# A weight-streaming recurrence on one core: a deeper ring, a different choice of resident chunks, an early preload, and four small moves

## The chip, the cores and the metric

One core of one Trainium2 chip. The metric is the device time of one execution in microseconds. Every run quoted here is in the fast state, so all of them may be compared; the sessions used different chips, so between sessions I compare the ratios to the kernel before, which ran in the same rounds. The kernel before takes 2934.2 us (median of 15 runs, 2922.1 to 2950.2).

## The reference, cut to what matters

Two independent computations on sequences of 2048 x 1024, in bf16. Part A is a gated long convolution through FFTs. Part B is a recurrent transformer: 64 segments of 32 tokens, each with 8 memory tokens in front that are the previous segment's output, so no segment can begin its projections of the memory rows before the last one is finished.

```python
for s in range(n_seg):                       # 64 segments
    h = concatenate([mem, x[s*32:(s+1)*32]])  # 8 + 32 tokens
    q = h @ Wq; k = h @ Wk; v = h @ Wv        # 32 heads of 128, each weight 8 MB
    p = softmax(mask(q @ k.T * scale))
    o = (p @ v) @ Wo                          # 8 MB
    mem = o[:8]; outs.append(o[8:])
```

The four weights are 32 MB together. The kernel keeps a part of them in on-chip memory and reads the rest again in each segment.

## The kernel before: the parts concerned

Part A has three stages: A1 (shifted product, first half of the FFT), A2 (34 units of complex product and second transform), A3 (last transform, gate, output). Part B cuts the weights into 64 chunks of 512 KB, 16 per matrix. 38 of them are resident; the other 26 are loaded anew in every segment, in order of use, by the SP queue into a ring of tiles. A load can only be issued when TensorE has finished with the tile that the ring gives it.

```python
NRES = 38; RING = 6
nres = [NRES // 4 + (1 if m < NRES % 4 else 0) for m in range(4)]   # Wq,Wk,Wv,Wo = 10,10,9,9
# ... the n resident chunks of a matrix are spread evenly over its 16 places ...
for m in range(4):                       # all residents first, ahead of the first segment
    for i in range(NCH):
        if i in res_slot[m]:
            nc.sync.dma_start(dst_view(res_tiles[m][:, res_slot[m][i], :], m), dram_chunk(m, i))

def wchunk(m, i):
    if i in res_slot[m]:
        return res_tiles[m][:, res_slot[m][i], :]
    t = ring.tile([128, CW], BF, tag="wring", name="wchunk")
    nc.sync.dma_start(dst_view(t[:], m), dram_chunk(m, i))
    return t[:]
# ... one segment: Q pass, K pass, V pass (beside it the scores and softmax), OTp, Wo pass ...
```

In the names of the profile, `acc` are the sums of the Q, K and V passes, `yacc` that of the Wo pass, `OTp` is attention times V, `PTs` the transposed softmax. In every fourth segment a pass works on two batches of rows (the "double" segments below).

In A2 each unit has four products on VectorE, then

```python
nc.gpsimd.tensor_tensor(out=Yre[P_], in0=pa[P_], in1=pb[P_], op=ALU.subtract)
nc.vector.tensor_tensor(out=Yim[P_], in0=pc[P_], in1=pd[P_], op=ALU.add)
```

## Time and profile before

| | before |
|---|---|
| median | 2934.2 us |
| profiled span, mean TensorE clock | 2931.5 us, 0.830 |
| first matmul of part B | at 282.8 us |
| end of the first segment (copy of its Y) | at 370.7 us |
| each of the other 63 segments | 40.35 us |
| from the last copy of Y to the end | 18.5 us |

The last three rows come from the starts of ScalarE's copies `Y_sb<-yacc` in the trace: 370.68 us for the first, 2912.96 us for the last, and their difference over 63. A segment is then cut by ScalarE's other events in it: end of the last copy of QA, of KA, starts of the two exponentials, first copy of OT, last copy of OT, end of the copy of Y. Means over the 63 segments, with TensorE's busy time, clock and DMA rate of the same stretches:

| stretch, before | us | PE busy us | clock | GB/s |
|---|---|---|---|---|
| Q: Y to end of QA | 10.98 | 6.85 | 0.883 | 369 |
| K: to end of KA | 8.43 | 6.76 | 0.854 | 359 |
| to first exponential | 4.62 | 4.14 | 0.963 | 381 |
| softmax, rest of V, to first OT | 7.21 | 3.58 | 0.873 | 377 |
| OTp | 2.81 | 2.78 | 0.521 | 283 |
| Wo: to Y | 6.30 | 5.82 | 0.746 | 234 |

The profile's own lines of before are shown in the prediction.

### The profile page before, as it was taken

Reading aid. Unit: us, or ns where it says so; the run is one execution under the profiler, and the core shown is the slowest. Engines: PE = TensorE matmul, PEld = TensorE weight load, DVE = VectorE, ACT = ScalarE, POOL = GpSimd, SP = SyncE. Lnnn points to the kernel's source line nnn. Section 1 sums busy time; section 2 is a strip of 40 time slices with the busy share of each in tenths; the row PEclk is TensorE's granted clock in tenths of the full one; section 3 lists DMA queues with packets and bytes.
Section 4 is the critical chain, followed back from the end, with each engine's and each line's share of the span. In section 5 each row is a group of like instructions: output and inputs, shape, how many; then the busy total and the mean of one; then the engine's idle time right before and its main releaser. Section 6 shows DMA issues by size and latency. Waiting matters only on the chain.

```text
span 2931.5 us, 80956 instructions
## 1 busy us (share of the span) xinstructions
PE 2079.3 (71%) x36052; PEld 1131.4 (39%) x36052; DVE 924.4 (32%) x1936; ACT 631.8 (22%) x1191; POOL 378.8 (13%) x714
## 2 busy tenths in 40 slices
PE   3665467686777778776867777777767786777775
PEld 1221234343444434343434444343434343443433
DVE  6895122232222322222322222222223222222222
ACT  6771111111111111111211111121112111111111
POOL 4141001001010101010010101010100101010101
PEclk9796689888887879788888888897979888897977
DMA  7886999989999999999999999999999999999996
GB/s 243 305 303 237 366 343 330 341 322 359 352 328 346 334 348 341 360 330 346 342 358 357 336 349 335 350 342 334 331 350 334 358 355 331 353 337 343 344 349 236
DMA packets 356981, 979.09 MB, mean 334 GB/s; under 512 B 42556, under 2 KB 47708, under 8 KB 356631
## 3 DMA queue, kind: packets, MB, share of 16 engines
q1 hardware_dynamic: 329896, 942.33, 88.5%
q0 software_dynamic: 21504, 21.04, 2.2%
q10 hardware_dynamic: 5232, 10.55, 1.2%
q8 instruction: 282, 4.62, 0.6%
q14 instruction: 67, 0.55, 0.1%
HBM read 940.19 MB, written 33.55 MB: 332 GB/s over the span
## 4 chain that ended last, share of the span: by engine, by line
PE 41%; DMA 32%; DVE 14%; ACT 4%; issue 2%; POOL 1%; SPq 0%; ACTq 0%; DVEq 0%; POOLq 0%
DMA wchunk<-in_B_Wq_dram 19%; PE acc L536 18%; PE yacc L561 11%; DMA wchunk<-in_B_Wk_dram 8%; PE OTp L698 4%; PE OTp L701 3%; PE qk_tp L548 3%; DMA wchunk<-in_B_Wv_dram 3%; DVE Ppads L592 2%; DVE ssum L590 2%; ACT KA_sb L541 2%; DVE mx L586 2%; ACT QA_sb L541 1%; DVE SA L582 1%; DVE SA L587 1%
## 5 line engine op out<-in xcount | busy, mean ns | idle before, releaser
L536 PE MATMUL acc<-wchunk,hT 128*32 128x512 bf16 x4864 | 583.7, 426 | 404.1 <-DMA wchunk<-in_B_Wq_dram 188.8
L536 PE MATMUL acc<-Wres,hT 128*32 128x512 bf16 x7424 | 771.8, 426 | 5.1 <-DMA Wres<-in_B_Wq_dram 5.1
L536 PEld LDWEIGHTS <-hT 128*32 128x32 bf16 x12288 | 393.6, 102 | 871.6 <-issue 646.1
L549 DVE COPY QT_sb<-qk_tp 128x1024 bf16<-128x1024 bf16 x80 | 55.3, 692 | 779.2 <-PE qk_tp L548 779.2
L698 PE MATMUL OTp<-PTs,VA_sb 32*128 32x64 bf16 x2048 | 202.1, 229 | 134.2 <-DVE PTs L687 132.6
L561 PEld LDWEIGHTS <-OT_sb 128*32 128x32 bf16 x8192 | 259.8, 121 | 80.9 <-issue 8.2
L561 PE MATMUL yacc<-Wres,OT_sb 128*32 128x256 bf16 x4608 | 289.1, 338 | 0.1
L561 PE MATMUL yacc<-wchunk,OT_sb 128*32 128x256 bf16 x3584 | 261.5, 352 | 6.7 <-DMA wchunk<-in_B_Wo_dram 3.9
L698 PEld LDWEIGHTS <-VA_sb 32*128 32x128 bf16 x2048 | 177.8, 118 | 184.9 <-issue 155.2
L536 PE MATMUL acc<-Wres,hTB 128*32 128x512 bf16 x1856 | 239.9, 386 | 0.0
L721 POOL DMA_DIRECT2D out_dram<-Y_sb x256 | 128.2, 508 | 841.1 <-ACT Y_sb L565 555.0
L541 ACT CAST QA_sb<-acc 128x512 bf16<-128x512 f32 x128 | 73.8, 588 | 673.5 <-PE acc L536 673.5
L605 POOL COPY hT<-XT_sb 128x192 bf16<-128x192 bf16 x64 | 22.2, 347 | 1437.0 <-issue 1053.1
L549 DVE COPY KT_sb<-qk_tp 128x1024 bf16<-128x1024 bf16 x80 | 55.2, 689 | 464.3 <-PE qk_tp L548 464.3
L701 PE MATMUL OTp<-PTs,VB_sb 32*128 32x64 bf16 x2048 | 193.5, 230 | 0.7
L541 ACT CAST KA_sb<-acc 128x512 bf16<-128x512 f32 x128 | 75.2, 588 | 489.4 <-PE acc L536 489.4
L701 PEld LDWEIGHTS <-VB_sb 32*128 32x128 bf16 x2048 | 179.5, 120 | 0.0
L536 PE MATMUL acc<-wchunk,hTB 128*32 128x512 bf16 x1216 | 168.8, 387 | 1.1 <-issue 1.1
L536 PEld LDWEIGHTS <-hTB 128*32 128x32 bf16 x3072 | 130.6, 98 | 70.8 <-issue 6.9
L704 ACT CAST OT_sb<-OTp 128x256 bf16<-128x256 f32 x256 | 94.3, 372 | 268.3 <-PE OTp L701 268.2
L612 DVE COPY hT<-mt_tp 128x64 bf16<-128x64 bf16 x64 | 12.3, 191 | 402.3 <-PE mt_tp L611 402.3
L726 POOL DMA_DIRECT2D out_dram<-YB_sb x256 | 126.6, 501 | 68.5 <-DMA out_dram<-Y_sb 30.6
(206 smaller groups left out, 2239.2 us busy)
## 6 DMA issues: line engine op xcount, KB each, us to landing
wchunk<-in_B_Wv_dram SPq DMA_DIRECT2D x448, 512.0 KB, 6.9
wchunk<-in_B_Wo_dram SPq DMA_DIRECT2D x448, 512.0 KB, 7.4
wchunk<-in_B_Wq_dram SPq DMA_DIRECT2D x384, 512.0 KB, 7.1
wchunk<-in_B_Wk_dram SPq DMA_DIRECT2D x384, 512.0 KB, 8.2
SK<-s_sb SPq DMA_DIRECT2D x16, 512.0 KB, 4.7
SU<-s_sb SPq DMA_DIRECT2D x16, 512.0 KB, 3.6
Kg<-SK ACTq DMA_DIRECT2D x32, 256.0 KB, 4.5
Ug<-SU SPq DMA_DIRECT2D x32, 256.0 KB, 5.0
```

The lines of the kernel that those rows point to most:

```text
L536: nc.tensor.matmul(accs[pi][g][32 * c:32 * c + 32, :], lhsT=hT_ap[:, kc, :], rhs=w[:, jl * 512:(jl + 1) * 512], start=(kc == 0), stop=(kc ...
L541: nc.scalar.copy(dst_sb[:, g * 512:(g + 1) * 512], accs[pi][g][:])
L548: nc.tensor.transpose(tp[:, idx * 128:(idx + 1) * 128], src_sb[:, idx * 128:(idx + 1) * 128], ident[:])
L549: nc.vector.tensor_copy(dst[:, :, :, col0:col0 + 32], tp[:].rearrange("p (i c r) -> p i c r", i=8, c=4))
L561: nc.tensor.matmul(accs[pi][32 * dq:32 * dq + 32, 0:256], lhsT=OTsrc[:, c, idx, :], rhs=w[:, hh * 1024 + dq * 256:hh * 1024 + (dq + 1) * 256],
L586: nc.vector.tensor_reduce(out=mx[:], in_=S3, op=ALU.max, axis=AX.X)
L590: nc.vector.tensor_reduce(out=ssum[:], in_=S3, op=ALU.add, axis=AX.X)
L698: nc.tensor.matmul(OTp[:, idx, :], lhsT=VA_sb[32 * c:32 * c + 32, col:col + 128], rhs=PTA[32 * c:32 * c + 32, idx, :], start=True, stop=False,
L701: nc.tensor.matmul(OTp[:, idx, :], lhsT=VB_sb[32 * c:32 * c + 32, col:col + 128], rhs=PTB[32 * c:32 * c + 32, idx, :], start=False, stop=True,
L704: nc.scalar.copy(OT_sb[:, c, :, :], OTp[:, :, 0:32])
L721: nc.gpsimd.dma_start(outb[SEG * s:SEG * s + 24, dq * 256:(dq + 1) * 256], Y_sb[32 * dq + 8:32 * dq + 32, :])
L726: nc.gpsimd.dma_start(outb[SEG * ss + 24:SEG * ss + 32, dq * 256:(dq + 1) * 256], YB_sb[32 * dq + 8 * jj:32 * dq + 8 * jj + 8, :])
```

## The change

Its intent: let the weight stream run further ahead (ring), take a chunk out of the stream just where it is awaited (split), use the idle DMA time in part A for resident weights (preload), and take small work off busy engines. Cut to its core:

```diff
-    RING = cfg.get("ring", 6)
+    RING = cfg.get("ring", 7)
-    nres = [NRES // 4 + (1 if m < NRES % 4 else 0) for m in range(4)]
+    nres = [11, 10, 8, 9]
...
+    N_PRE = 20                      # 11 Wq and 9 Wk chunks
+    with tc.tile_pool(name="b_pre", bufs=1) as prepool:
+        pre_tile = prepool.tile([128, N_PRE, 2048], BF, name="Wpre")
+        ... a_kernel(..., after_a1=lambda: b_preload(...))   # loads without a wait: they land early in A
...
-    for m in range(4):              # all residents ahead of segment 0
+    load_rest(0); load_rest(1)      # and load_rest(2) after the first K pass,
+                                    # load_rest(3) ahead of the first Wo pass
...
-            load_rows(Qall[:, t, :], q, t, 0, nc.gpsimd)      # in A1
+                load_rows(Qall[:, st, :], q, st, 0, nc.sync)  # in A2
-            nc.vector.tensor_tensor(out=Yim[P_], in0=pc[P_], in1=pd[P_], op=ALU.add)
+            nc.gpsimd.tensor_tensor(out=Yim[P_], in0=pc[P_], in1=pd[P_], op=ALU.add)
...
+        oeng = nc.sync if s == n_seg - 1 else nc.gpsimd       # last outputs by SP
```

Also: four small copies of shift weights are dropped (a matmul reads them strided), one buffer less for K rows in A1, two more in A3. Per segment the stream still has 26 chunks, but Wq, Wk, Wv, Wo now take 5, 6, 8, 7 of them instead of 6, 6, 7, 7.

More of the change, by code (lines that the diff above doesn't have):

```diff
@@ L19, with a_kernel @@
 NEG = -1.0e9
-def a_kernel(ctx: ExitStack, tc, q, k, v, shift_k, ssm_k, ssm_D, outa, dbg_stop=None):
+def a_kernel(ctx: ExitStack, tc, q, k, v, shift_k, ssm_k, ssm_D, outa, dbg_stop=None, after_a1=None):
     nc = tc.nc
@@ L41, in a_kernel @@
     ones_row = const.tile([1, 128], BF, name="ones_row")
-    shflat = const.tile([1, 4096], BF, name="shflat")
     SH = [const.tile([128, 1024], BF, name=f"SH{j}") for j in range(4)]
-    shrows = [const.tile([1, 1024], BF, name=f"shrow{j}") for j in range(4)]
-    Drow = const.tile([1, 1024], BF, name="Drow")
-    Qall = const.tile([128, 16, 1024], BF, name="Qall")
     def rows_view(ap2d, t):
@@ L59, in load_rows @@
             eng.dma_start(dst[113:128, :], rv[112:127])
-    nc.sync.dma_start(shflat[:], shift_k.rearrange("(o d) j -> o (d j)", o=1))
-    nc.sync.dma_start(Drow[:], ssm_D.rearrange("(o d) -> o d", o=1))
     ksn_cm = tc.tile_pool(name="a1_ksn", bufs=1)
@@ L65, in a_kernel @@
     KS = ksn.tile([128, 8, 2048], BF, name="KS_nat")
+    shflat = ksn.tile([1, 4096], BF, name="shflat")
+    Drow = ksn.tile([1, 1024], BF, name="Drow")
+    nc.sync.dma_start(shflat[:], shift_k.rearrange("(o d) j -> o (d j)", o=1))
+    nc.sync.dma_start(Drow[:], ssm_D.rearrange("(o d) -> o d", o=1))
     for db in range(8):
@@ L204, in a_kernel @@
         io = c1.enter_context(tc.tile_pool(name="a1_io", bufs=3))
-        k0pool = c1.enter_context(tc.tile_pool(name="a1_k0", bufs=6))
+        k0pool = c1.enter_context(tc.tile_pool(name="a1_k0", bufs=5))
         wk = c1.enter_context(tc.tile_pool(name="a1_wk", bufs=3))
@@ L210, in a_kernel @@
         for j in range(4):
-            nc.vector.tensor_copy(shrows[j][:], shflat[:].rearrange("o (d j) -> o d j", j=4)[:, :, j])
             pt = ps_big.tile([128, 1024], F32, tag="big", name="sh_ps")
@@ L214, in a_kernel @@
                 nc.tensor.matmul(pt[:, hf * 512:(hf + 1) * 512], lhsT=ones_row[0:1, :],
-                                 rhs=shrows[j][0:1, hf * 512:(hf + 1) * 512], start=True, stop=True)
+                                 rhs=shflat[0:1, :].rearrange("o (d j) -> o d j", j=4)[:, hf * 512:(hf + 1) * 512, j],
+                                 start=True, stop=True)
             nc.scalar.copy(SH[j][:], pt[:])
@@ L264, in a_kernel @@
         return
+    if after_a1 is not None:
+        after_a1()
+    qpool = ctx.enter_context(tc.tile_pool(name="a_q", bufs=1))
+    Qall = qpool.tile([128, 16, 1024], BF, name="Qall")
     def valid_re(k1):
@@ L355, in a_kernel @@
         for st in range(NS):
+            if st < 16:
+                load_rows(Qall[:, st, :], q, st, 0, nc.sync)
             cur = nxt
@@ L369, in a_kernel @@
     with ExitStack() as c3:
-        io = c3.enter_context(tc.tile_pool(name="a3_io", bufs=4))
+        io = c3.enter_context(tc.tile_pool(name="a3_io", bufs=6))
         wk = c3.enter_context(tc.tile_pool(name="a3_wk", bufs=3))
@@ L383, in a_kernel, with b_plan, b_dram_chunk, b_preload @@
             nc.sync.dma_start(rows_view(outa, t), ot[:])
-def b_kernel(ctx: ExitStack, tc, x, mem0, Wq, Wk, Wv, Wo, outb, n_seg, cfg=None):
+def b_plan(cfg=None):
+    cfg = dict(cfg or {})
+    NRES = cfg.get("nres", 38)
+    CW = cfg.get("cw", 2048)
+    NCH = 8 * (4096 // CW)
+    nres = [11, 10, 8, 9]
+    plan = []
+    g = 0
+    for m in range(4):
+        n = nres[m]
+        slots = {}
+        for i in range(NCH):
+            if ((i + 1) * n) // NCH > (i * n) // NCH:
+                slots[i] = g
+                g += 1
+        plan.append(slots)
+    return plan, g
+def b_dram_chunk(Wq, Wk, Wv, Wo, m, i, CW=2048):
+    CPK = 4096 // CW
+    HPC = CW // 1024
+    if m == 3:
+        return Wo.rearrange("(hp hh e) d -> hp e hh d", hh=HPC, e=128)[i]
+    W = (Wq, Wk, Wv)[m]
+    return W.rearrange("(kc p) (hf c) -> kc hf p c", p=128, hf=CPK)[i // CPK, i % CPK]
+def b_preload(tc, Wq, Wk, Wv, Wo, pre_tile, n_pre, cfg=None):
+    nc = tc.nc
+    cfg = dict(cfg or {})
+    CW = cfg.get("cw", 2048)
+    plan, tot = b_plan(cfg)
+    k = 0
+    for m in range(4):
+        for i, gidx in plan[m].items():
+            if gidx < n_pre:
+                dst = pre_tile[:, gidx, :]
+                if m == 3:
+                    dst = dst.rearrange("p (hh d) -> p hh d", hh=CW // 1024)
+                nc.sync.dma_start(dst, b_dram_chunk(Wq, Wk, Wv, Wo, m, i, CW))
+                k += 1
+def b_kernel(ctx: ExitStack, tc, x, mem0, Wq, Wk, Wv, Wo, outb, n_seg, cfg=None, pre=None):
     nc = tc.nc
@@ L457, in b_kernel, with res_ap @@
     Wo_v = Wo.rearrange("(hp hh e) d -> hp e hh d", hh=HPC, e=128)
-    nres = [NRES // 4 + (1 if m < NRES % 4 else 0) for m in range(4)]
-    res_slot = []
-    res_tiles = []
-    for m in range(4):
-        n = nres[m]
-        slots = {}
-        cnt = 0
-        for i in range(NCH):
-            if ((i + 1) * n) // NCH > (i * n) // NCH:
-                slots[i] = cnt
-                cnt += 1
-        assert cnt == n
-        res_slot.append(slots)
-        res_tiles.append(wres.tile([128, max(n, 1), CW], BF, name=f"Wres{m}"))
+    plan, n_total_res = b_plan(cfg)
+    pre_tile, n_pre = (pre if pre is not None else (None, 0))
+    n_rest = n_total_res - n_pre
+    rest_tile = wres.tile([128, max(n_rest, 1), CW], BF, name="Wres") if n_rest > 0 else None
+    res_slot = plan
+    def res_ap(gidx):
+        if gidx < n_pre:
+            return pre_tile[:, gidx, :]
+        return rest_tile[:, gidx - n_pre, :]
     def dram_chunk(m, i):
-        if m == 3:
-            return Wo_v[i]
-        return (Wq_v, Wk_v, Wv_v)[m][i // CPK, i % CPK]
+        return b_dram_chunk(Wq, Wk, Wv, Wo, m, i, CW)
     def dst_view(ap, m):
@@ L481, in dst_view, with load_rest @@
         return ap
-    for m in range(4):
+    def load_rest(m):
         for i in range(NCH):
-            if i in res_slot[m]:
-                nc.sync.dma_start(dst_view(res_tiles[m][:, res_slot[m][i], :], m), dram_chunk(m, i))
+            if i in res_slot[m] and res_slot[m][i] >= n_pre:
+                nc.sync.dma_start(dst_view(res_ap(res_slot[m][i]), m), dram_chunk(m, i))
+    load_rest(0)
+    load_rest(1)
     RELAYOUT = cfg.get("relayout", False)
@@ L500, in wchunk @@
         if i in res_slot[m]:
-            return res_tiles[m][:, res_slot[m][i], :]
+            return res_ap(res_slot[m][i])
         if cfg.get("fake_resident"):
-            return res_tiles[m][:, 0, :]
+            return res_ap(0)
         t = ring.tile([128, CW], BF, tag="wring", name="wchunk")
@@ L646, in b_kernel @@
         qkv_pass(kpairs, 1)
+        if s == 0:
+            load_rest(2)
         VA_sb = qk.tile([128, 1024], BF, tag="qk_sb", name="VA_sb")
@@ L710, in b_kernel @@
             VB_cur[0] = VB_new
+        if s == 0:
+            load_rest(3)
         Y_sb = act.tile([128, 256], BF, tag="Y_sb", name="Y_sb")
@@ L719, in b_kernel @@
             hT = hT_next
+        oeng = nc.sync if s == n_seg - 1 else nc.gpsimd
         for dq in range(4):
-            nc.gpsimd.dma_start(outb[SEG * s:SEG * s + 24, dq * 256:(dq + 1) * 256], Y_sb[32 * dq + 8:32 * dq + 32, :])
+            oeng.dma_start(outb[SEG * s:SEG * s + 24, dq * 256:(dq + 1) * 256], Y_sb[32 * dq + 8:32 * dq + 32, :])
         if j == NB - 1:
+            oeng = nc.sync if b == n_blk - 1 else nc.gpsimd
             for dq in range(4):
@@ L725, in b_kernel @@
                     ss = NB * b + jj
-                    nc.gpsimd.dma_start(outb[SEG * ss + 24:SEG * ss + 32, dq * 256:(dq + 1) * 256],
-                                        YB_sb[32 * dq + 8 * jj:32 * dq + 8 * jj + 8, :])
+                    oeng.dma_start(outb[SEG * ss + 24:SEG * ss + 32, dq * 256:(dq + 1) * 256],
+                                   YB_sb[32 * dq + 8 * jj:32 * dq + 8 * jj + 8, :])
     if cfg.get("dbg_pools"):
@@ L759 @@
     outb = out[0, :, 1024:2048]
-    with ExitStack() as ctx_a:
-        a_kernel(ctx_a, tc, A_q[0], A_k[0], A_v[0], A_shift_k, A_ssm_k, A_ssm_D, outa)
-    with ExitStack() as ctx_b:
-        b_kernel(ctx_b, tc, B_x[0], B_mem0[0],
-                 B_Wq.rearrange("d h e -> d (h e)"), B_Wk.rearrange("d h e -> d (h e)"),
-                 B_Wv.rearrange("d h e -> d (h e)"), B_Wo.rearrange("h e d -> (h e) d"),
-                 outb, n_seg)
+    Wq2 = B_Wq.rearrange("d h e -> d (h e)")
+    Wk2 = B_Wk.rearrange("d h e -> d (h e)")
+    Wv2 = B_Wv.rearrange("d h e -> d (h e)")
+    Wo2 = B_Wo.rearrange("h e d -> (h e) d")
+    N_PRE = 20
+    with tc.tile_pool(name="b_pre", bufs=1) as prepool:
+        pre_tile = prepool.tile([128, N_PRE, 2048], BF, name="Wpre")
+        with ExitStack() as ctx_a:
+            a_kernel(ctx_a, tc, A_q[0], A_k[0], A_v[0], A_shift_k, A_ssm_k, A_ssm_D, outa,
+                     after_a1=lambda: b_preload(tc, Wq2, Wk2, Wv2, Wo2, pre_tile, N_PRE))
+        with ExitStack() as ctx_b:
+            b_kernel(ctx_b, tc, B_x[0], B_mem0[0], Wq2, Wk2, Wv2, Wo2, outb, n_seg, pre=(pre_tile, N_PRE))
 _INS = ['A_q', 'A_k', 'A_v', 'A_shift_k', 'A_ssm_k', 'A_ssm_D', 'B_x', 'B_mem0', 'B_Wq', 'B_Wk', 'B_Wv', 'B_Wo', 'B_seg_len']
```

## The prediction

> **What bounds the kernel now.** I read the page first: its busy shares and slices, then the chain that ended last, then the stretches and the waits.
>
> ```profile
> PE 2079.3 (71%) x36052; PEld 1131.4 (39%) x36052; DVE 924.4 (32%) x1936; ACT 631.8 (22%) x1191; POOL 378.8 (13%) x714
> ...
> PE 41%; DMA 32%; DVE 14%; ACT 4%; issue 2%; POOL 1%; SPq 0%; ACTq 0%; DVEq 0%; POOLq 0%
> ```
>
> No engine is full, and the chain of the end is split: 41% TensorE, 32% waiting for DMA, 14% VectorE. So this is a chain of steps that follow each other, with a DMA stream beside it that is almost but not quite the bound. The stretches (columns: bounds, length, then busy us of PE, PEld, DVE, ACT, POOL, then TensorE clock, DMA share, GB/s) show the program's three parts:
>
> ```profile
> 30.00:35.00 5.00, 0.00 (x0) 0.00 (x0) 0.00 (x0) 4.98 (x8) 0.00 (x0) 1.00 0.00 0
> 55.00:125.00 70.00, 45.82 (x198) 20.81 (x197) 69.97 (x117) 65.37 (x71) 6.45 (x12) 0.79 0.86 300
> 140.00:235.00 95.00, 62.76 (x382) 22.34 (x380) 92.79 (x169) 67.59 (x131) 43.25 (x38) 0.93 0.79 269
> ...
> 282.00:369.00 87.00, 40.13 (x632) 20.24 (x636) 12.08 (x26) 10.01 (x19) 1.32 (x4) 0.64 0.95 351
> 369.00:2913.00 2544.00, 1887.35 (x34698) 1051.18 (x34686) 698.23 (x1494) 449.77 (x925) 280.28 (x583) 0.84 0.95 343
> 2913.00:2932.00 19.00, 0.04 (x1) 0.00 (x0) 0.00 (x0) 0.61 (x2) 9.87 (x20) 0.63 0.04 7
> ```
>
> Part A (to about 280 us) is bound by VectorE: 69.97 of 70 us and 92.79 of 95 us. Early in it, while ScalarE makes sine tables, DMA stands still. Then 282 to 369 us is the first segment of part B, with loads of resident weights. Then 63 equal segments take 2544 us: 2544/63 = 40.4 us each, 87% of the program. What ends last in a segment I read from the waits and from the slices around the output projection ("yacc"):
>
> ```profile
> PE acc L536 <- DMA wchunk<-in_B_Wq_dram: 188.8, 223, 3.1
> PE OTp L698 <- DVE PTs L687: 132.6, 60, 4.4
> PE acc L536 <- DMA wchunk<-in_B_Wv_dram: 120.7, 138, 2.4
> PE acc L536 <- DMA wchunk<-in_B_Wk_dram: 75.2, 59, 35.7
> ```
>
> ```profile
> 1177.00:1178.00 1.00, 1.00 (x28) 1.00 (x25) 0.22 (x1) 0.09 (x1) 0.00 (x0) 0.50 1.03 377
> 1178.00:1179.00 1.00, 1.00 (x24) 0.80 (x25) 0.23 (x1) 0.72 (x2) 0.00 (x0) 0.50 0.59 223
> 1179.00:1180.00 1.00, 1.00 (x24) 0.73 (x20) 0.22 (x1) 0.02 (x1) 0.00 (x0) 0.50 0.23 76
> 1180.00:1181.00 1.00, 1.00 (x28) 0.77 (x20) 0.00 (x0) 0.00 (x0) 0.00 (x0) 0.50 0.81 121
> 1181.00:1182.00 1.00, 1.00 (x28) 0.72 (x24) 0.00 (x0) 0.00 (x0) 0.00 (x0) 0.50 1.06 395
> ```
>
> A segment streams 26 chunks of 512 KB through a ring of 6 slots. At the start of the Wo pass the ring is full (nothing was consumed during softmax), so the stream stops: three slices moved 223 + 76 + 121 KB-per-us where about 385 was usual, a loss of (1155 - 420)/385 = 1.9 us. Right after it the Wq pass needs chunks that are only now being asked for, and TensorE waits: 188.8 us over 64 segments is 2.95 us each. Nothing else can run then, so this wait is on the path. The Wv wait (1.9 us each) mostly isn't: softmax runs beside it, and OTp afterwards still waits 132.6/64 = 2.1 us for PTs.
>
> **What the Trainium skill says.** "Perfetto Trace Analysis", Optimization Strategy: the same gap repeating on the engine that should be saturated can mean too few buffers for the next tile. The trace agrees: the dip returns in each segment I looked at (1056, 1140, 1178, 1218 us). "DMA: Bandwidth & Descriptors", Anatomy of one DMA, gives about 2.0 us fixed plus bytes/436e3 us; for 524,288 bytes that is 3.2 us. The fastest ring load here landed in 3.6 us, so a chunk asked for late costs some 2 us before the stream is full again. "TensorE: Matmul & The Clock Gate", HAM oscillation: waits for DMA that outlast the monitor's window drop the array to half clock. The trace has a clock of 0.50 in the K pass after a Wq wait, and 0.84 on the mean, so shorter waits should not cost clock, and may gain some. "SBUF — State Buffer", SBUF: two separate sides: a VectorE op with two SBUF inputs and a GpSimd op that reads SBUF lock each other out of a shared port. That is Yim on VectorE (median 418 ns, longest 1328) against Yre on GpSimd (1152 ns); the change puts both on GpSimd.
>
> **The change part by part.**
>
> 1. *Ring 6 to 7, and residents 10,10,9,9 to 11,10,8,9.* Streamed per segment: Wq 5, Wk 6, Wv 8, Wo 7 (was 6,6,7,7). Bytes are the same. But before the last Wq chunk, the stream had to bring the seventh Wo chunk (no slot was left for it) and six Wq; now five Wq. Two chunks earlier at 524,288/385e3 = 1.36 us each is 2.7 us. The wait was 2.95 us, and every fourth segment (two batches per pass) had only about 0.9, so I take 2.2 us of the 2.7. The Wv end comes after 19 chunks instead of 20 counted from the Wo pass, one chunk earlier, while its consumer comes 2.2 us earlier: it loses some 0.8 us of a 2.1 us slack, so nothing on the path. Check by the other limit: 26 chunks at 385 GB/s are 35.4 us, plus about 2 us of restart at each Wo pass and small output writes: 37.8 us. The path says 40.4 - 2.2 = 38.2 us, above it. Gain: 63 x 2.2 = about 138 us.
>
> 2. *Preload of 20 resident chunks, issued by SP right after the KS loads* (seen in the built program's order: ahead of the first K load). 20 x 0.524 MB = 10.5 MB at some 400 GB/s is 26 us, from about 12 to 39 us, where DMA now carries Q (4.2 MB) and then nothing. The first K load now leaves at 39.3 us, behind the sine tables, so part A starts on time within 2 us.
>
> 3. *First segment.* From about 283 us until its Wo pass, the queue carries now 38 residents + 6 Wk + 7 Wv + 7 Wo = 58 chunks (the six Wq were fetched during A2). After: 5 Wq + 1 resident Wk + 6 + (8 + 8) Wv + (9 + 7) Wo = 44. The stretch 305 to 310 us ran at 416 GB/s with deep queues, about 1.3 us a chunk: 14 x 1.3 = 18 us. K no longer waits behind all residents (its longest wait was 35.7 us), so I take 20 us.
>
> 4. *A2: Yim moves to GpSimd, 34 units.* VectorE per unit is now 4 x 0.60 + 0.42 = 2.8 us; after 2.4 us. GpSimd becomes 2 x 1.16 = 2.3 us and ScalarE is at about 2.1 plus issues. All three are near each other and z waits for Yim, so I take 0.12 us a unit: 4 us, not the 14 of VectorE alone. Q moves to SP in the late A1 and A2, where DMA was 0.56 to 0.9 busy, in place of six ring chunks: nothing.
>
> 5. *Small ones.* shrow copies dropped (8.8 us of VectorE, before the sine tables): hidden by the preload. k0 6 to 5: four live tiles and one ahead, nothing. A3 with six zt buffers: 1 us. Last outputs by SP: GpSimd issued 20 at 0.5 us in the 19 us tail, SP needs 0.35: 3 us.
>
> Sum: 138 + 20 + 5 + 3 = 166; 2934 - 166 = 2768, say 2770 us.
>
> **The rivals.** (a) *The DMA stream was already the bound* (share 0.95): ring and split then buy only what idle time there is. Against it: the share counts packets in flight, while 343 GB/s is well below the 385 of the busy slices. If true the period falls by perhaps 0.7 us: 44 + 28 saved, 2860 us. (b) *The wait moves*: eight Wv chunks delay OTp, or seven Wo chunks aren't in at the Wo pass. For it: the Wv wait is 120.7 us already, and some segments (1061 to 1102) had no PTs wait at all. Then half of the 2.2 us returns: 2840 us. (c) *Better than the path says*: Q pass without gaps keeps the clock at full, and the K pass (5.6 us at half clock in one segment) shortens by 1 to 2 us; then the stream's 37 us is the bound: 2700 us. (d) *Part A suffers*: the preload holds back K, or Q loads on SP hold back the SU and SK stores behind them. At most some 10 us.
>
> **Range and chances.** The sum depends on one term, saved time per segment, between 0.9 us (2854) and 3.4 us (2696), with 28 us of rather safe savings. Range 2700 to 2850. "Faster" by 2% needs under 2875 us, that is only 0.5 us per segment beside the 28: 0.93. Same 0.06, slower 0.01.
>
> **What would show it.** In the changed profile: segments of about 38.2 us; the Wq wait from 189 us to under 80; the dip at the start of the Wo pass under 1 us; mean GB/s in B near 360; DMA busy between 12 and 39 us; K pass of the first segment done some 40 us earlier relative to its first load; A2 a few us shorter with GpSimd near full. I am wrong if the Wq wait shrinks but Wv, Wo or PTs waits grow by as much, or if the waits fall and segments still take 40 us.

## The result, and the profile after

The changed kernel takes 2702.1 us (median of 11 runs, 2692.6 to 2711.3). The ratio to the kernel before is 0.9209, 95% interval 0.919 to 0.9228: 7.9% less time. Ratios here are the mean time of one kernel's fast runs over that of the other's in the same rounds, so not quite the ratio of the medians that I quote. The prediction was 2770 us, range 2700 to 2850: the range holds the result by 2 us, at its low edge, and the point was 68 us too high.

The page of the changed kernel, busy times and the chain that ended last:

```profile
PE 2000.2 (74%) x36052; PEld 1129.9 (42%) x36052; DVE 904.7 (34%) x1898; ACT 629.7 (23%) x1191; POOL 397.5 (15%) x712
...
PE 38%; DMA 35%; DVE 13%; ACT 3%; issue 2%; POOL 1%; ACTq 0%; SPq 0%; DVEq 0%; POOLq 0%
```

TensorE has as many matmuls as before, 36052, but is busy for 2000.2 instead of 2079.3 us, and its mean granted clock rose from 0.830 to 0.862. The DMA share of the chain did not fall; it rose from 32 to 35%. The stretches of the changed kernel (columns as in the prediction):

```profile
30.00:35.00 5.00, 0.00 (x0) 0.00 (x0) 0.00 (x0) 4.98 (x9) 0.00 (x0) 1.00 1.03 409
140.00:235.00 95.00, 70.54 (x390) 25.38 (x385) 82.96 (x137) 69.00 (x132) 82.89 (x74) 0.93 0.76 256
340.00:2683.00 2343.00, 1801.86 (x34626) 1045.77 (x34630) 698.23 (x1494) 447.25 (x924) 281.25 (x583) 0.87 0.99 372
2684.00:2694.00 10.00, 0.00 (x0) 0.00 (x0) 0.00 (x0) 0.39 (x2) 0.00 (x0) 0.76 0.06 12
```

The reader is to see three things. The 5 us that moved nothing now move 409 GB/s: the preload. In A2 GpSimd is busy for 82.89 of 95 us instead of 43.25. And the 63 segments run at 372 instead of 343 GB/s, with clock 0.87 instead of 0.84. The waits of TensorE (total us, times, longest):

```profile
PE acc L580 <- DMA wchunk<-in_B_Wv_dram: 150.1, 192, 4.3
PE OTp L744 <- DVE PTs L733: 100.5, 53, 3.5
PE acc L580 <- DMA wchunk<-in_B_Wk_dram: 84.2, 155, 2.1
PE acc L580 <- DMA wchunk<-in_B_Wq_dram: 66.1, 93, 5.6
```

The Wq wait fell from 188.8 to 66.1 us and the Wv wait rose from 120.7 to 150.1 us. The Wk wait rose too: the 75.2 us of before hold one of 35.7 us in the first segment, so it was 39.5 in the other 63, and is 84.2 now. PTs, which OTp awaits after V, fell from 132.6 to 100.5 us: a bit of the slack beside softmax was used. The start of one Wo pass, slice by slice, as in the prediction:

```profile
1227.00:1228.00 1.00, 1.00 (x26) 0.98 (x23) 0.06 (x1) 0.37 (x1) 0.00 (x0) 0.50 1.05 387
1228.00:1229.00 1.00, 1.00 (x23) 0.71 (x24) 0.39 (x2) 0.37 (x1) 0.00 (x0) 0.50 0.96 352
1229.00:1230.00 1.00, 1.00 (x28) 0.72 (x24) 0.00 (x0) 0.00 (x0) 0.00 (x0) 0.50 0.76 250
1230.00:1231.00 1.00, 1.00 (x24) 0.75 (x20) 0.00 (x0) 0.00 (x0) 0.00 (x0) 0.50 1.09 293
1231.00:1232.00 1.00, 1.00 (x32) 0.78 (x24) 0.00 (x0) 0.00 (x0) 0.00 (x0) 0.65 0.83 293
```

The stream no longer falls to 76 GB/s. At the prediction's 385 GB/s four slices move 1540; here 352 + 250 + 293 + 293 = 1188, so this dip costs (1540 - 1188)/385 = 0.9 us instead of 1.9.

Where the 238.3 us between the two profiled spans (2931.5 and 2693.2) came from:

| stretch | before | after | difference | predicted |
|---|---|---|---|---|
| start to first matmul of B | 282.8 | 280.8 | -2.0 | -5 |
| first segment, from there to its Y | 87.9 | 59.2 | -28.7 | -20 |
| 63 segments | 63 x 40.35 | 63 x 37.20 | -198.5 | -138 |
| tail after the last Y | 18.5 | 9.5 | -9.0 | -3 |

And within a segment:

| stretch, after | us | PE busy us | clock | GB/s |
|---|---|---|---|---|
| Q | 7.39 | 5.62 | 0.993 | 364 |
| K | 8.42 | 6.21 | 0.960 | 405 |
| to first exponential | 4.87 | 4.56 | 0.919 | 407 |
| to first OT | 7.25 | 3.55 | 0.853 | 385 |
| OTp | 2.77 | 2.73 | 0.535 | 354 |
| Wo | 6.50 | 5.94 | 0.737 | 303 |

All of the gain is in the Q stretch: 10.98 to 7.39 us, while the others moved by 0.25 us or less. Of these 3.59 us, 1.23 are TensorE's own busy time (6.85 to 5.62), and 2.36 are idle time. Busy time times clock fell as well, from 6.85 x 0.883 = 6.05 to 5.62 x 0.993 = 5.58, so by this estimate some 0.5 of the 1.23 us are not the clock's; the ends of matmuls are modelled in the profile, where at full clock four in a row stand with 0.40 us and eight with 0.62 (1226 us of the kernel before), so work in pieces counts for more.

### The profile page after: what moved, and what is told of

The parts are those of the page before. It is cut to its first block, busy times and chain, and to the rows that moved or that the text cites.

```text
span 2693.2 us, 80982 instructions
## 1 busy us (share of the span) xinstructions
PE 2000.2 (74%) x36052; PEld 1129.9 (42%) x36052; DVE 904.7 (34%) x1898; ACT 629.7 (23%) x1191; POOL 397.5 (15%) x712
## 4 chain that ended last, share of the span: by engine, by line
PE 38%; DMA 35%; DVE 13%; ACT 3%; issue 2%; POOL 1%; ACTq 0%; SPq 0%; DVEq 0%; POOLq 0%
PE acc L580 16%; DMA wchunk<-in_B_Wk_dram 11%; PE yacc L605 11%; DMA wchunk<-in_B_Wq_dram 11%; DMA wchunk<-in_B_Wv_dram 10%; PE OTp L744 4%; PE OTp L747 3%; PE qk_tp L592 3%; DVE Ppads L636 2%; DVE ssum L634 2%; DVE mx L630 2%; ACT KA_sb L585 2%; DMA wchunk<-in_B_Wo_dram 1%; DVE SA L626 1%; DVE SA L631 1%
## 5 line engine op out<-in xcount | busy, mean ns | idle before, releaser
L580 PE MATMUL acc<-wchunk,hT 128*32 128x512 bf16 x4864 | 585.1, 402 | 321.7 <-DMA wchunk<-in_B_Wv_dram 150.1
L580 PE MATMUL acc<-Wpre,hT 128*32 128x512 bf16 x5120 | 462.5, 388 | 0.2 <-issue 0.2
L605 PEld LDWEIGHTS <-OT_sb 128*32 128x32 bf16 x8192 | 266.6, 122 | 102.4 <-issue 27.7
L605 PE MATMUL yacc<-Wres,OT_sb 128*32 128x256 bf16 x4608 | 294.7, 343 | 0.1
L744 PE MATMUL OTp<-PTs,VA_sb 32*128 32x64 bf16 x2048 | 196.6, 226 | 108.7 <-DVE PTs L733 100.5
L580 PE MATMUL acc<-Wres,hT 128*32 128x512 bf16 x2304 | 245.6, 405 | 0.3 <-issue 0.3
L744 PEld LDWEIGHTS <-VA_sb 32*128 32x128 bf16 x2048 | 172.9, 116 | 150.1 <-issue 83.2
L580 PE MATMUL acc<-wchunk,hTB 128*32 128x512 bf16 x1216 | 175.2, 384 | 3.3 <-issue 3.3
L580 PE MATMUL acc<-Wpre,hTB 128*32 128x512 bf16 x1280 | 155.4, 383 | 0.0
```

Source lines behind the costliest of these rows:

```text
L580: nc.tensor.matmul(accs[pi][g][32 * c:32 * c + 32, :], lhsT=hT_ap[:, kc, :], rhs=w[:, jl * 512:(jl + 1) * 512], start=(kc == 0), stop=(kc ...
L605: nc.tensor.matmul(accs[pi][32 * dq:32 * dq + 32, 0:256], lhsT=OTsrc[:, c, idx, :], rhs=w[:, hh * 1024 + dq * 256:hh * 1024 + (dq + 1) * 256],
L744: nc.tensor.matmul(OTp[:, idx, :], lhsT=VA_sb[32 * c:32 * c + 32, col:col + 128], rhs=PTA[32 * c:32 * c + 32, idx, :], start=True, stop=False,
```

## The experiments

Three theories of the steady gain were on the table at first. **A**: ring and split each bring the last Wq chunk one chunk earlier, in wait and in the clock that goes with it. **B**: only the deeper ring counts. **C**: something else in the change. After the first four runs I took A at its narrowest, to have it refuted or not: the arrival of chunks sets the passes, and the clock is of no account; its rival, again called C in the expectation of e10, is that a good part is clock. Twelve kernels were run, each with three rounds.

### Ring and split, undone and alone

```diff
 e1:  RING = cfg.get("ring", 7)   ->   cfg.get("ring", 6)            # in the changed kernel
 e2:  nres = [11, 10, 8, 9]       ->   [10, 10, 9, 9]                # in the changed kernel
 e3:  both of these
 e4b: RING 6 -> 7 and nres -> [11, 10, 8, 9]                         # in the kernel before, nothing else
```

> The changed kernel with the ring put back from 7 to 6 slots; the residents stay 11,10,8,9. Theory A (both parts bring the last Wq chunk one chunk earlier each, and each is worth about half of the 3.15 us that a segment lost): about 1.6 us more per segment, 63 x 1.6 = 100 us, so about 2800 us, with the time from Y to the last QA copy near 9 us (7.4 in the changed kernel, 11.0 before). Theory B (only the deeper queue counts, since it keeps the DMA stream running, and the split moves nothing): all 200 us come back, about 2900 us.

> The changed kernel with the residents put back to 10,10,9,9; the ring stays at 7. Theory A: about 2800 us, as with the ring alone undone. Theory B (only the ring counts): 2702 us, the same as the changed kernel, since the bytes of a segment are the same.

> The changed kernel with both put back (ring 6, residents 10,10,9,9); what is left is the preload, Yim on GpSimd, the deeper zt buffers and the last outputs by SP. Theories A and B: the segments go back to 40.3 us, so 2702 + 200 = about 2900 us, some 35 us under the kernel before. Theory C (the segments became faster for another reason, such as where the tiles lie in SBUF or outputs by SP): well under 2850 us.

> The kernel before with only ring 7 and residents 11,10,8,9: no preload and nothing else of the change. Theories A and B: segments of 37.2 us, so 2934 - 200 = about 2735 us. Theory C: over 2850 us.

| | median us | ratio to before | us per segment | Q stretch | Q clock | K stretch GB/s |
|---|---|---|---|---|---|---|
| before | 2931.9 | | 40.35 | 10.98 | 0.883 | 359 |
| e3 (ring 6, even) | 2894.3 | 0.9869 (0.9849 to 0.9888) | 40.37 | 10.84 | 0.906 | 363 |
| e1 (ring 6, split) | 2798.8 | 0.9544 (0.9526 to 0.9562) | 38.90 | 8.71 | 0.983 | 385 |
| e2 (ring 7, even) | 2788.9 | 0.9514 (0.949 to 0.9538) | 38.75 | 9.26 | 0.953 | 388 |
| e4b (ring 7, split, nothing else) | 2746.9 | 0.9375 (0.9351 to 0.94) | 37.33 | 7.46 | 0.996 | 407 |
| changed kernel | 2702.1 | 0.9209 (0.919 to 0.9228) | 37.20 | 7.39 | 0.993 | 405 |

So A is right that the two parts add: 1.6 us per segment from the ring, 1.5 from the split, 3.2 from both (the per-segment column). B falls: without the split, 2788.9 and not 2702. C falls: without both, the segments are at 40.37 us, as if nothing had been changed; everything else in the change together gives the rest, 2931.9 - 2894.3 = 38 us, all outside the steady segments. The segments of e4b show from the other side that the steady gain needs nothing but these two lines. The traces show the shift itself: SP issues a segment's last Wq chunk on the mean 0.3 us before the copy of the previous Y starts in the kernel before, and 0.2 (e3), 1.1 (e2), 1.5 (e1), 1.9 (e4b) and 2.0 us (changed kernel) before it. What is left open is the size: a chunk takes 1.36 us of the stream (524,288 bytes at 385 GB/s), yet each part gave about 1.55, and the clock of the Q stretch rose with each.

### The clock alone

In the kernel before, matmuls of zero weights are put ahead of the streamed Wq chunks, in segments with one batch of rows. They add zero to the same sums, so the result is right; loads, ring and split stay as before.

```diff
                 w = wchunk(m, CPK * kc + hf)
+                if m == 0 and len(pairs) == 1 and kc > 0 and (CPK * kc + hf) not in res_slot[m]:
+                    for jx in range(8):
+                        nc.tensor.matmul(accs[0][hf][...], lhsT=zer[:],     # zer: all zeros
+                                         rhs=res_tiles[0][:, 0, 0:512], start=False, stop=False, ...)
```

> The kernel before, with eight matmuls of zero weights put ahead of each streamed Wq chunk's own (segments with one pair only; result stays right), to keep the clock up in the Q pass without changing the loads. Theory A (the arrival of the last Wq chunk sets the end of the Q pass, the clock does not matter there): clock in the Q phase from 0.88 to above 0.95, time unchanged within 15 us of the kernel before. Rival C (part of the gain was clock: 1.2 us of TensorE's busy time per Q pass): 48 x 1.2 = 58 us faster, 2875 us.

Measured: 2875.7 us (2871.0 to 2883.4), ratio 0.9803, interval 0.9768 to 0.9838. More work for TensorE, and the program is 56 us faster: the figure of the clock rival, and the narrow A's "unchanged within 15 us" falls. That the figure came out is partly luck. It counted 48 segments at 1.2 us; by their place in a group of four the segments gained 1.6, 1.1, 0.8 and -0.1 us, and the one with 0.8 is the double one, which has no fillers of its own. The Q stretch went from 10.98 to 10.20 us at clock 0.981, the K stretch from 8.43 to 8.18 at 0.969, a segment from 40.35 to 39.50. The 63 segments of this kernel, beside those of the kernel before (the prediction's line with 0.84 and 343):

```profile
367.00:2856.00 2489.00, 1927.08 (x36573) 1103.34 (x36566) 698.32 (x1494) 448.28 (x926) 281.60 (x583) 0.88 0.95 350
```

The stream's 350 instead of 343 GB/s is only the same bytes in a shorter time (343 x 40.35/39.50 = 350). What the clock does in the kernel before can be seen in single slices of a Q pass with its waits:

```profile
1225.00:1226.00 1.00, 0.00 (x0) 0.00 (x0) 0.00 (x0) 0.00 (x0) 1.00 (x3) 1.00 1.05 274
1226.00:1227.00 1.00, 0.83 (x12) 0.33 (x12) 0.00 (x0) 0.00 (x0) 0.00 (x1) 1.00 0.94 336
1227.00:1228.00 1.00, 0.55 (x12) 0.35 (x15) 0.00 (x0) 0.00 (x0) 0.00 (x0) 1.00 1.02 403
1228.00:1229.00 1.00, 0.59 (x16) 0.19 (x7) 0.00 (x0) 0.00 (x0) 0.00 (x0) 1.00 1.03 403
1229.00:1230.00 1.00, 0.31 (x4) 0.02 (x4) 0.00 (x0) 0.00 (x0) 0.00 (x0) 1.00 1.10 367
1230.00:1231.00 1.00, 0.70 (x12) 0.24 (x11) 0.00 (x0) 0.00 (x0) 0.00 (x0) 1.00 0.96 389
1231.00:1232.00 1.00, 0.31 (x6) 0.18 (x3) 0.00 (x0) 0.58 (x1) 0.00 (x0) 0.80 1.01 414
1232.00:1233.00 1.00, 1.00 (x12) 0.30 (x10) 0.00 (x0) 0.00 (x0) 0.00 (x0) 0.50 1.03 401
```

From 1225 to 1231 us TensorE is busy for 2.98 of 6 us, in pieces, with no gap over 1.22 us. Then the clock is 0.50, and the K pass runs at half speed.

A useful comparison follows: e10 and e4b both have a Q clock of 0.98 to 1.00 and a K clock of 0.96 to 0.97, and differ in ring and split. Their segments are 39.50 and 37.33 us: 2.17 us, which is what the prediction gave the earlier chunks (2.2). The Wq wait alone proves little: in e10 it is 78.5 instead of 188.8 us with the loads unchanged, as the fillers stand in its place. The fillers of e10 cost TensorE busy time of their own (7.95 us in the Q stretch instead of 6.85), so the division into 0.85 of clock and 2.17 of arrival is not exact.

### The two limits, each by itself

Wrong result in both: the matmuls read a resident chunk in the place of every streamed one, e8 without issuing the loads, e9 with all of them still issued, but not held up by TensorE.

```diff
 e8:  if i not resident:  return res_ap(0)              # no load at all
 e9:  nc.sync.dma_start(dst_view(t[:], m), dram_chunk(m, i))
-     return t[:]
+     return res_ap(0)
```

> The changed kernel, but no chunk is streamed: every streamed chunk's place is taken by one resident chunk (wrong result on purpose). Theory A (in the changed kernel the stream still sets the Q, K and V passes, only the stretch from OTp to Y is TensorE's own): TensorE's 28.6 us per segment at clock 0.87 are 24.9 us at full clock, with some 5 us of evictions and softmax that it must wait for 30 to 32 us per segment, so 2250 to 2400 us, clock above 0.93. Rival D (the dependent chain is the bound now and the stream is hidden): segments of 36 to 37 us, 2640 to 2700 us.

> The changed kernel, still loading all 26 chunks per segment into the ring, but the matmuls read a resident chunk (wrong result on purpose), so the stream is never held back by TensorE. Theory A (the stream's rate of about 405 GB/s with all slots open is its own limit): 13.6 MB per segment at 405 GB/s are 33.7 us, 2460 to 2530 us, about 405 GB/s through the whole of part B. Rival (the 372 GB/s seen now is what this stream can do): 36.6 us per segment, 2650 to 2700 us.

Measured: e8 2389.1 us, ratio 0.8144 (0.8117 to 0.817), 32.46 us per segment; e9 2538.9 us, ratio 0.8652 (0.8618 to 0.8685). The stretches of e8, of e9 up to its last Y, and of e9's stream that runs on after it:

```profile
331.00:2376.00 2045.00, 1650.58 (x34658) 1030.45 (x34646) 698.19 (x1494) 436.49 (x924) 280.72 (x583) 0.88 0.03 6
```

```profile
330.00:2430.00 2100.00, 1678.68 (x34646) 1042.09 (x34646) 698.39 (x1494) 437.66 (x926) 282.56 (x583) 0.87 1.03 397
2430.00:2535.00 105.00, 0.00 (x0) 0.00 (x0) 0.00 (x0) 0.36 (x2) 0.00 (x0) 0.52 0.98 379
```

So the chain of work alone needs 32.5 us per segment. A's time for e8 holds, but its clock of over 0.93 does not: it was 0.87, as OTp and Wo ran at 0.55 and 0.71 without any stream too. The stream alone moves 397 GB/s, not the 405 that I expected, and the 2538.9 us lie just outside A's 2460 to 2530. At 397 GB/s 26 x 524,288 bytes take 34.3 us. In the changed kernel a segment takes 37.2 us, 2.9 above the slower of the two; that this is each holding up the other is my reading. Rival D (the chain was the bound, the stream hidden) falls, and so does "372 GB/s is what the stream can do". In e8 TensorE's wait for PTs is 314.9 us instead of 100.5: without the stream, softmax is what it waits for.

### The clock beside softmax

If OTp and Wo ran at full clock, their 9.27 us at a clock of 0.5 to 0.7 would shrink. In the changed kernel, idle matmuls are put ahead of the last streamed Wv chunks (zero weights) and ahead of OTp (into a spare bank).

```diff
+ if m == 2 and len(pairs) == 1 and kc > 3 and not resident: 8 matmuls of zero weights into accs[0][hf]
+ warm = ps_t.tile([128, 512], F32, tag="tp", name="warm")
+ 4 matmuls warm <- ident, VA_sb;  4 matmuls warm <- ident, Ppads
```

> The changed kernel, with idle matmuls beside softmax (eight of zero weights ahead of each of the last streamed Wv chunks, eight into a spare bank before OTp; result stays right), so that OTp and the Wo pass start at full clock. Theory A (that stretch is TensorE's own at a clock of 0.68 now, 9.3 us; the stream has 2 us of stall there to give back): 1 to 2 us per segment, 2580 to 2650 us. Rival D2 (the stream of 26 chunks at 372 GB/s is the whole period already): unchanged, 2690 to 2715 us, with longer Wq waits.

Measured: 2713.1 us (2705.8 to 2717.1), ratio 0.9244 (0.9211 to 0.9277). The mean clock of the program rose from 0.862 to 0.935, the highest of all runs, and nothing was gained. OTp and Wo together went from 9.27 to 7.50 us; but the stretch up to OTp went from 7.25 to 8.48 and the Q stretch from 7.39 to 8.41. Its waits:

```profile
PE acc L584 <- DMA wchunk<-in_B_Wq_dram: 103.2, 148, 5.7
```

The Wq wait grew from 66.1 to 103.2 us: what TensorE wins in Wo it waits for in Q. A's 2580 to 2650 falls. D2's range holds, but not its reason, as the stream alone did 397 GB/s and not 372 (e9). It is not a pure test, as the 1.2 us ahead of OTp are at least partly the fillers' own time.

### Further along the same way

Three variants of the changed kernel, to see whether another step of split, or bytes in place of depth, gives more.

```diff
 e13: nres = [11, 10, 8, 9]  ->  [11, 11, 7, 9]
 e14: nres = [11, 10, 8, 9]  ->  [11, 10, 7, 10]
 e15: nres = [11, 10, 8, 9]  ->  [11, 11, 8, 9],  NRES 38 -> 39,  RING 7 -> 6
```

> The changed kernel with residents 11,11,7,9: one streamed chunk more moves from Wk to Wv. Theory A2 (up to the end of the K pass each chunk taken out of the stream is 1.3 to 1.5 us earlier, and Wv's arrival has 1.6 us of slack left before PTs): 0.5 to 1.3 us per segment, 2620 to 2670 us. Rival (Wv now sets OTp's start): 2695 to 2740 us.

> The changed kernel with residents 11,10,7,10: one streamed chunk moves from Wo to Wv, so the seven slots hold all six streamed Wo chunks and the next segment's first Wq chunk when the Wo pass begins. Theory A2: both Wq and Wk come one chunk earlier than in the changed kernel, Wv's last one no later relative to the Wo pass: 0.8 to 1.5 us per segment, 2610 to 2655 us. Rival (Wv sets OTp's start): 2695 to 2740 us.

> The changed kernel with a ring slot given to a 39th resident chunk (ring 6, residents 11,11,8,9): 25 chunks streamed. Theory A (open slots count more than bytes: a slot is worth 1.55 us per segment, a chunk less to stream 1.3 us and only up to the passes after it): 2700 to 2740 us. Rival (bytes are the bound, depth isn't): one chunk of 26 less, 2600 to 2640 us.

Measured: e13 2699.7 us, ratio 0.9222 (0.92 to 0.9244); e14 2691.9 us, 0.9187 (0.9146 to 0.9229); e15 2734.1 us, 0.9346 (0.9321 to 0.9371). The first two cannot be told from the changed kernel (0.919 to 0.9228). I had given A2 the better chances there, and it fell: the K stretch of e13 is 1.15 us shorter, the Q stretch of e14 0.77 us, and both give it back ahead of OTp (7.25 to 7.97 and 7.98 us) and in smaller pieces. The waits of e14:

```profile
PE acc L580 <- DMA wchunk<-in_B_Wv_dram: 214.5, 270, 3.0
PE acc L580 <- DMA wchunk<-in_B_Wk_dram: 95.9, 172, 2.4
PE OTp L744 <- DVE PTs L733: 51.4, 22, 2.7
```

Wv is now 214.5 us, PTs down to 51.4: the slack beside softmax is used up. e15 shows that a ring tile is worth more than a chunk less to load: 4% fewer bytes, and 37.94 us per segment instead of 37.20. No version was shown to beat the changed kernel.

### Preload and Yim undone

Two parts that lie in different stretches of the trace, undone in one kernel.

```diff
-    N_PRE = 20; ... a_kernel(..., after_a1=...) ... pre=(pre_tile, N_PRE)
+    a_kernel(...); b_kernel(...)          # all residents loaded in B, each matrix before its first use
-            nc.gpsimd.tensor_tensor(out=Yim[P_], in0=pc[P_], in1=pd[P_], op=ALU.add)
+            nc.vector.tensor_tensor(out=Yim[P_], in0=pc[P_], in1=pd[P_], op=ALU.add)
```

> The changed kernel with two parts of it undone that lie in different stretches of the trace: no preload (all 38 resident chunks are loaded in part B, still each matrix just before its first use), and Yim back on VectorE. As predicted: part A's A2 stage 4 us longer; the first segment 20 us longer, now 20 chunks more at 1.3 us less what they hid behind; 2720 to 2730 us. Rival E (the first segment gained from the lazy order of loads, not from the preload): first segment within 8 us of the changed kernel's, about 2708 us. Rival F (the preload costs part A what it saves later): below 2700 us.

Measured: 2724.1 us (2719.0 to 2735.8), ratio 0.9303 (0.9276 to 0.933): 27 us slower than the changed kernel by the ratios. ScalarE's copies of K in the first segment, before, after, and in e12:

```profile
347.82 0.58 ACT L541 CAST KA_sb<-acc 128x512 bf16<-128x512 f32 x1 [45.53 <-PE acc L536]
```

```profile
298.64 0.58 ACT L585 CAST KA_sb<-acc 128x512 bf16<-128x512 f32 x1 [6.44 <-PE acc L580]
```

```profile
317.98 0.59 ACT L585 CAST KA_sb<-acc 128x512 bf16<-128x512 f32 x1 [19.21 <-PE acc L580]
```

Before, ScalarE had stood for 45.53 us, as the K chunks came behind all residents. From the first matmul of B to the first Y it is 87.9 us before, 81.2 in e12 (277.7 to 358.9) and 59.2 after. So the preload gave 22.0 us. The other 6.7 are not the order of loads alone, as e12 also has ring and split: e4b, with nothing but these two, takes 83.9 (284.8 to 368.7). That leaves 3.9 for ring and split and 2.7 for the order. The division is rough, as B starts at another time in each (282.8, 284.8, 277.7 and 280.8 us; its first Y is at 370.7, 368.7, 358.9 and 340.0). Rival E, for which the order did it all, falls, and F with it. The preload may have a price: B starts 3.1 us later in the changed kernel than in e12, whose A2 is longer; the changed kernel waits 5.61 us for its first Wq chunk there. Why this chunk is late was not tried.

A2, from the first product to the end of the last Yim, took 96.2 us before (138.8 to 235.0), 94.7 in e12 and 90.3 after. Yim on GpSimd is worth 4.4 us. Its instructions late in A2, before and after (min/median/max ns, first and last start):

```profile
L336 DVE TENSOR_TENSOR Yim<-pc,pd x6: 406/408/418, 221.4 to 234.6; 128x512 bf16<-128x512 bf16 x4, 64x512 bf16<-64x512 bf16 x2
```

```profile
L337 POOL TENSOR_TENSOR Yim<-pc,pd x5: 1141/1148/1153, 219.7 to 229.3; 128x512 bf16<-128x512 bf16 x3, 64x512 bf16<-64x512 bf16 x2
```

The same add takes 1148 instead of 408 ns and still the stage is shorter, since VectorE was the full engine.

## Why the prediction was right, and where its sizes were off

- **The bound, right.** The wait for Wq at the start of a segment was on the path, and ring and split shorten it: 188.8 to 66.1 us, predicted under 80. Other waits took back a part but not "as much": Wk's grew by 44.7 us in the 63 segments, Wv's by 29.4, and PTs' fell by 32.1. Each part alone gave half (e1, e2), as "two chunks earlier" says.
- **The steady term, too small: 138 predicted, 198 measured.** The step that failed is in "the change part by part": "so I take 2.2 us of the 2.7". At like clocks the runs show about that, 2.17 us (e10 against e4b, not an exact division). What was missing in the sum is TensorE's own clock. The prediction said that shorter waits "should not cost clock, and may gain some", put the gain into rival (c), and did not add it. e10 shows 0.85 us per segment from filling alone, without a change of loads. How the measured 3.15 us divide exactly stays open. The range held this by 2 us only, so being inside it is partly luck. Its end points are also some 4 us off in the prediction's own sum: with 28 us of other savings, 0.9 and 3.4 us per segment give 2849 and 2692, not 2854 and 2696.
- **"Check by the other limit", wrong.** It took 385 GB/s as the ceiling of the stream and came to 37.8 us, above the 37.2 that were measured. The ceiling was only that of slices with six tiles: the K stretch reached 405, and the stream by itself 397 GB/s over 2100 us (e9), 34.3 us per segment.
- **First segment, too small: 20 predicted, 28.7 measured.** The count of chunks was of the right kind (18 us; preload 22.0 in e12). For the new order the prediction added some 2 us, and the runs give 2.7; the rest, some 3.9, goes with ring and split (e4b) and was not in the sum. This division is rough.
- **Part A.** The preload starts A on time within 2 us: right, the first product of A2 is at 140.1 instead of 138.8. A2: 4 predicted, 4.4 shown for Yim and 5.9 in all. But B's first matmul is only 2.0 us earlier, as it waits for the first Wq chunk for 5.61 us.
- **Tail, too small: 3 predicted, 9.0 measured.** The issues went as predicted. The last two lines of each (start, length):

```profile
2913.62 1.99 POOL L721 DMA_DIRECT2D out_dram<-Y_sb  x4 [39.51 <-ACT YB_sb L565]
2915.61 7.88 POOL L726 DMA_DIRECT2D out_dram<-YB_sb  x16
```

```profile
2684.14 1.56 SPq L770 DMA_DIRECT2D out_dram<-Y_sb  x4
2685.80 5.34 SPq L776 DMA_DIRECT2D out_dram<-YB_sb  x16
```

  That is 9.87 and 6.90 us, 3.0 apart. The rest is after the last issue: before, it ended at 2923.5 and the program at 2931.5, 8.0 us; after, 2691.1 and 2693.2, 2.1 us. No run changes this alone, but the traces' records of DRAIN, which the views leave out, show what ended last: before, the last packet of a store was through at 2924.2 us and SP was done at 2925.5, but GpSimd's own closing DRAIN, 8.8 us long, ran to 2930.7. In e4b, where GpSimd still issues the last outputs, it is 8.8 us again and the tail 18.6. In the changed kernel GpSimd's DRAIN (8.0 us) is over at 2654.0, long before the end.
- **The rivals.** (a) fell: the stream had room, 343 to 372 GB/s with the same bytes. (b) fell for this change, but holds for one step more (e13, e14). (c) was right in its direction and its number, 2700, but not in its place: the K stretch did not shorten (8.43 to 8.42 us, as it now waits more for Wk), the gain is in Q, and the stream alone needs 34.3 us and not 37. (d) fell within its 2 us.

## What to carry to other kernels

Where a stream of weights and a chain of work hold each other up, run each by itself: the two times (here 34.3 and 32.5 us) show what is left to win, which a busy share of 0.95 does not. Count the clock as a term of its own when a change closes small gaps on TensorE: filling them alone gave 56 us here; but once the stream is near its limit, a clock of 0.935 instead of 0.862 gave nothing. And move a load to where its consumer has slack (Wv beside softmax) until that slack is used: the first step gave some 1.5 us per segment, the second none.

## What the Trainium skill lacked or had wrong

- "TensorE: Matmul & The Clock Gate", HAM oscillation: the working rule there is to have no idle gaps of over about 3.4 us. That rule is not enough here, and the page has no figure for shorter gaps. In the Q pass shown no gap was over 1.22 us, TensorE was busy for half of 6 us, and the clock still fell to 0.50 (1225 to 1232 us of the kernel before; in the whole of it no wait for Wq was over 3.1 us). Filling such gaps raised the clock of the Q stretch from 0.883 to 0.981 (e10). Whether the busy share or the number of gaps decides was not separated.
- "DMA: Bandwidth & Descriptors", Where 436 GB/s comes from: it says that about 358 GB/s bind for loads from device memory into on-chip memory. Taken alone this misleads for a program on one core, for which the page also has a measured 425 GB/s. This core, with no other in the program, moved 397 GB/s over 2100 us (e9) and 409 in the preload.
- No page that I read has it: how far ring depth and split move the rate of such a stream. With like bytes and a DMA share of 0.99 to 1.02 in all of them, the K stretch moved 363 (ring 6, even), 385 (ring 6, split), 388 (ring 7, even) and 405 GB/s (ring 7, split). As two of these have the same ring, depth alone does not set it.
- No page that I read has it: GpSimd ends with a DRAIN of 8.0 to 8.8 us in the kernel before, e4b and the changed kernel. Where GpSimd issues the last 20 output stores, it ends after they have landed, and from the last issue to the end of the program it takes 8.0 us; with these stores on SP it is 2.1 us.
